# One attention and channel-mix kernel on one core: a new order of all engines, new buffer places, and casts moved to GpSimd

## The chip, the core and the metric

The kernel runs on one core of a Trainium2 chip. The core has five instruction streams that run side by side and meet through semaphores: TensorE (PE, matrix products; its weight loads are listed as PEld), VectorE (DVE), ScalarE (ACT), GpSimd (POOL) and SyncE (SP), which here issues nearly all transfers. Each stream runs its instructions in the order in which they were emitted; an instruction that waits holds up everything behind it on the same stream.

The metric is the device time of one execution in microseconds (us). The kernel before took 166.66 us, the median of three runs (166.03 to 167.26).

## The reference: what is computed

Windowed attention with a few sink keys, then an RWKV channel mix on its output, for 4 batches, 8 heads, 768 positions and heads of 64.

```python
scores = (1 / sqrt(64)) * q @ k.T
keep = (key < 4) | ((0 <= query - key) & (query - key < 128))
a = softmax(where(keep, scores, -1e9))
x = concat_heads(a @ v)                      # (4, 768, 512)
...
x_prev = x shifted by one position, 0 at the start
xk = mu_k * x + (1 - mu_k) * x_prev          # xr likewise with mu_r
k = relu(xk @ w_k)                           # 512 -> 1024
v = (k * k) @ w_v                            # 1024 -> 512
out = sigmoid(xr @ w_r) * v
```

Inputs and output are float32; the kernel computes its products in bfloat16.

## The kernel before, in words

The 4 x 768 positions are cut into 12 units of 256 positions, three to a batch (U = 12; T is the unit's place in its batch). Each unit goes through four stages.

*prepare* (lines 531 to 684). SP loads 256 positions of q, k and v in float32 (lines 307, 317 and 337, two transfers of 256 KB for each tensor). Each half is cast to bfloat16: `kb` and `qb` (op at line 547; the copies at lines 536 and 543), `vb` (op at line 648, copy at line 646). The halves of q and k are then transposed, either on PE (line 576) with a copy out of PSUM (line 589), or, for k of units 4 to 11 and q of units 8 to 11, by a DMA transpose that SP issues (line 562). For the first unit of a batch the four sink keys are gathered (`ksink`, POOL, line 670), and the sink values as well (lines 676 and 680).

*attend* (lines 687 to 828). For each pair of heads PE makes scores (line 721), ACT the exponential (line 775), DVE the product with a window mask (line 789); units 0 and 1 have the mask added on PE instead (line 728, from `bias`). PE multiplies with v (line 808, sink part at line 763), DVE takes the reciprocal of the sums (line 822) and scales (line 825) into `x`.

*mix* (lines 831 to 897). `x` is transposed on PE (line 849, copied out at line 858) or by DMA (units 9 to 11, line 869). DVE forms the difference to the position before (`td`, line 877) and from it `xk` and `xr` (line 888).

*ffn* (lines 927 to 1015). PE makes the keys (line 939), which go through a relu (ACT line 949 or DVE line 953) and a square (DVE line 963 or ACT line 967), the gate (line 979, ACT tanh at line 985) and the values (line 997); DVE joins both (line 1006) and SP stores. The last 128 positions are cut in two (lines 909 to 924). The weights are loaded once (line 354) and cast in ten pieces (lines 501, 505 and 507).

None of this is emitted as it is written. `Plan.op` only notes each of the 1052 operations with its number; `Plan.run` then emits them in the order of a written list, `ORDER`. Since each engine is in order, `ORDER` sets the order on every engine and in SP's queue. A negative entry is a filling matmul on zeros (line 1018), which does no work of the kernel and keeps PE active. `SLOTS` says, in order of the operations, which buffer of its pool each tile takes. `CHOICE` says which engine runs an operation that several engines can run (220 of the operations: casts, copies out of PSUM, relus and squares); one that is not listed stays on the engine that its `P.op` names.

```python
if i in CHOICE:
    engine = CHOICE[i]
    cost, emit, port = alts[engine]
...
for i in ORDER:
    if i < 0:
        self.fill(banks[(-1 - i) % len(banks)], 512 if -i <= len(banks) else 128)
    else:
        self.ops[i]["emit"]()
```

Numbers that the change and the prediction speak of: 0 to 3 are the loads of q and k of unit 0, 8 and 9 those of q of unit 1, 10 and 11 the loads of w_k, 82 to 89 POOL's constants (82 the identity, 87 the head mask, 88 the sink sums, 84 and 83 the biases), 92 to 101 the casts of the weights, 249 the first scores of unit 2, 212 the second transpose of x of unit 1, and 219 and 223 key products of unit 0's ffn. `TOGETHER`, `KD`, `QD`, `XD`, `BIAS` and the other settings are the same before and after.

Of the kernel before, what the change touches and what calls it, by code (L numbers as in the profile page):

```python
# [18 lines left out]
    92: "ACT", 93: "ACT", 94: "ACT", 95: "ACT", 97: "ACT", 100: "ACT", 102: "DVE", 105: "DVE",  # L19
    110: "DVE", 111: "DVE", 114: "ACT", 115: "DVE", 139: "POOL", 142: "POOL", 145: "POOL", 148:  # L20
    "DVE", 150: "DVE", 151: "ACT", 152: "ACT", 154: "DVE", 161: "DVE", 191: "DVE", 193: "DVE",
    194: "DVE", 197: "DVE", 199: "DVE", 200: "DVE", 203: "DVE", 204: "DVE", 213: "DVE", 230:
    "ACT", 234: "ACT", 273: "DVE", 276: "DVE", 279: "DVE", 282: "DVE", 285: "ACT", 286: "ACT",
    298: "DVE", 306: "DVE", 315: "ACT", 354: "DVE", 364: "ACT", 365: "DVE", 367: "DVE", 383:
    "ACT", 387: "ACT", 436: "DVE", 439: "DVE", 444: "DVE", 445: "DVE", 467: "ACT", 475: "ACT",
    514: "DVE", 516: "DVE", 521: "DVE", 524: "ACT", 525: "ACT", 546: "ACT", 550: "ACT", 554:
    "ACT", 558: "ACT", 595: "DVE", 598: "DVE", 603: "ACT", 604: "ACT", 606: "DVE", 634: "ACT",
    681: "DVE", 682: "DVE", 691: "DVE", 700: "ACT", 704: "ACT", 708: "ACT", 755: "DVE", 759:
    "DVE", 760: "ACT", 772: "DVE", 781: "ACT", 785: "ACT", 789: "ACT", 834: "DVE", 836: "DVE",
    837: "DVE", 853: "ACT", 856: "DVE", 857: "ACT", 860: "DVE", 861: "ACT", 904: "DVE", 906:  # L30
    "DVE", 910: "DVE", 912: "DVE", 913: "DVE", 929: "ACT", 933: "ACT", 940: "DVE", 941: "ACT",
    994: "DVE", 995: "ACT", 999: "ACT", 1003: "ACT", 1007: "ACT", 1022: "DVE", 1026: "DVE",
    1034: "DVE", 1035: "ACT",
# [1041 lines left out]
```

## Time and profile before

| what | value |
|---|---|
| median of three runs | 166.66 us (166.03 to 167.26) |
| span of the profiled execution, first to last instruction | 164.3 us |
| that execution's own time | not on the page; the three runs lie 1.7 to 3.0 us above the span |
| ACT casts of q, k and v | 31, of 0.62 to 0.77 us on the mean by group |
| DVE casts of q, k and v | 38, about 0.42 us each |
| POOL casts of q, k and v | 3, all between 12 and 16 us |
| filling matmuls | 30 |
| DMA, mean over the span | 211 GB/s |

A row of a group names the line, the engine, the operation, what it writes and reads, and the count; then the busy time in us and the mean of one in ns; then the engine's idle time ahead of it and what ended it. A row of the timeline begins with the start and the length in us; several instructions of the same kind in a row are merged, with their count. The chain of waits is followed back from the last instruction: each piece is what the next had to wait for. A row of stages gives, for each engine, the busy time within that stretch and the instructions in it.

### The profile page before, as it was taken

What the parts mean: (1) busy time and instruction counts of PE and PEld (TensorE: products, weight loads), DVE (VectorE), ACT (ScalarE), POOL (GpSimd) and SP (SyncE); (2) the same over time, 40 slices, a digit from 0 to 9 for tenths busy, and PEclk for the clock granted to TensorE, in tenths of its full rate; (3) what the DMA queues carried; (4) which work ended last, traced back from release to release, by engine and by line L of the source; (5) the groups of instructions that cost most, each with busy time, mean ns of one, the idle gap of its engine ahead of it and who ended that gap; (6) DMA issues with size and microseconds to landing.
All of it is one profiled execution on the core that took longest, in us unless ns stands there. A gap on an engine that the chain in (4) does not pass through costs nothing.

```text
span 164.3 us, 4195 instructions
## 1 busy us (share of the span) xinstructions
PE 158.4 (96%) x1603; PEld 102.6 (62%) x1603; DVE 145.4 (89%) x381; ACT 131.2 (80%) x218; POOL 13.5 (8%) x38
## 2 busy tenths in 40 slices
PE   6999889999999999999999999999999999999992
PEld 2455568866467587577566775856575765664851
DVE  5259999999999999989999999999999999789752
ACT  3277999999999999999999999997668759163240
POOL 6409300010000000060000000000000000000000
PEclk9999999999999999999999999999999999999999
DMA  4999999999969896999999887986996955077743
GB/s 120 247 305 311 348 335 355 301 354 210 228 154 270 135 240 148 234 198 167 224 216 157 188 156 163 235 146 150 199 123 136 362 149 200 0 90 297 262 185 128
DMA packets 79042, 34.60 MB, mean 211 GB/s; under 512 B 67112, under 2 KB 73520, under 8 KB 79024
## 3 DMA queue, kind: packets, MB, share of 16 engines
q1 hardware_dynamic: 79008, 34.35, 86.3%
q8 instruction: 12, 0.20, 0.6%
q14 instruction: 6, 0.05, 0.1%
q10 hardware_dynamic: 16, 0.00, 0.0%
HBM read 24.12 MB, written 6.29 MB: 185 GB/s over the span
## 4 chain that ended last, share of the span: by engine, by line
PE 79%; ACT 8%; SPq 4%; DMA 3%; issue 2%; DVE 1%; POOL 1%; DVEq 0%; ACTq 0%; POOLq 0%
PE bank L997 23%; PE bank L939 23%; PE bank L979 12%; PE bank L808 6%; PE sc L721 6%; SPq L337 3%; DMA qs<-in_q_dram 3%; PE bank L576 2%; ACT e L775 2%; PE bank L849 2%; ACT rl L949 1%; PE bank L763 1%; ACT qt L589 1%; PE bank L909 1%; PE bank L1018 1%
## 5 line engine op out<-in xcount | busy, mean ns | idle before, releaser
L775 ACT ACTIVATE e<-sc 128x1024 bf16<-128x1024 f32 (+1 forms) x48 | 46.1, 994 | 1.8 <-PE sc L721 1.7
L939 PE MATMUL bank<-xk,wk_sb 128*128 128x256 bf16 x384 | 47.1, 273 | 0.0
L997 PE MATMUL bank<-wv_h,kk 128*128 128x512 bf16 x184 | 43.1, 379 | 0.1
L939 PEld LDWEIGHTS <-wk_sb 128*128 128x128 bf16 x384 | 36.4, 98 | 7.4 <-issue 0.4
L949 ACT ACTIVATE rl<-bank 128x512 bf16<-128x512 f32 x40 | 24.2, 625 | 8.6 <-PE bank L939 7.1
L997 PEld LDWEIGHTS <-kk 128*128 128x128 bf16 x184 | 17.1, 98 | 17.8 <-issue 0.4
L789 DVE TENSOR_TENSOR e<-e,mask 128x1024 bf16<-128x1024 bf16 (+1 forms) x40 | 25.4, 642 | 0.7 <-ACT e L775 0.5
L979 PE MATMUL bank<-wr_sb,xr 128*128 128x512 bf16 x96 | 23.7, 379 | 0.0
L888 DVE SCALAR_TENSOR_TENSOR xk<-td,mu_all,xt 128x256 bf16<-128x256 bf16 x48 | 22.4, 483 | 0.3
L888 DVE SCALAR_TENSOR_TENSOR xr<-td,mu_all,xt 128x256 bf16<-128x256 bf16 x48 | 22.1, 475 | 0.2
L967 ACT ACTIVATE kk<-rl 128x512 bf16<-128x512 bf16 x29 | 18.3, 664 | 4.2 <-DVE rl L953 4.0
L985 ACT ACTIVATE th<-bank 128x512 f32<-128x512 f32 x24 | 15.1, 646 | 5.7 <-PE bank L979 5.7
L825 DVE TENSOR_TENSOR x<-bank,rec 128x256 bf16<-128x256 f32 x48 | 19.2, 416 | 0.4
L808 PE MATMUL bank<-vb,e 128*128 128x65 bf16 x352 | 16.6, 194 | 0.0
L1006 DVE SCALAR_TENSOR_TENSOR w<-th,bank 128x512 f32<-128x512 f32 x19 | 13.0, 682 | 3.6 <-issue 1.8
L808 PEld LDWEIGHTS <-e 128*128 128x128 bf16 x352 | 13.6, 97 | 3.5
L979 PEld LDWEIGHTS <-xr 128*128 128x128 bf16 x96 | 8.8, 98 | 8.6 <-issue 0.2
L721 PE MATMUL sc<-qt,kt 64*128 64x128 bf16 (+1 forms) x256 | 13.9, 238 | 0.0
L721 PEld LDWEIGHTS <-kt 64*128 64x128 bf16 x256 | 8.9, 94 | 5.7 <-issue 3.1
L1018 PE MATMUL bank<-warm 128*128 128x512 bf16 x30 | 10.6, 484 | 1.1 <-DVE warm L1038 1.1
L877 DVE TENSOR_TENSOR td<-xt 128x512 bf16<-128x512 bf16 x24 | 10.3, 428 | 0.7 <-ACT xt L858 0.5
L589 ACT COPY qt<-bank 128x512 bf16<-128x512 bf16 x15 | 9.4, 643 | 1.0 <-PE bank L576 1.0
(74 smaller groups left out, 161.7 us busy)
## 6 DMA issues: line engine op xcount, KB each, us to landing
ks<-in_k_dram SPq DMA_DIRECT2D x24, 256.0 KB, 4.7
qs<-in_q_dram SPq DMA_DIRECT2D x24, 256.0 KB, 4.4
vs<-in_v_dram SPq DMA_DIRECT2D x24, 256.0 KB, 4.4
out_dram<-w SPq DMA_DIRECT2D x19, 256.0 KB, 2.7
w<-in_moe_w_k_dram SPq DMA_DIRECT2D x2, 1024.0 KB, 10.4
w<-in_moe_w_v_dram SPq DMA_DIRECT2D x2, 1024.0 KB, 9.3
w<-in_moe_w_r_dram SPq DMA_DIRECT2D x1, 1024.0 KB, 9.7
out_dram<-ob SPq DMA_DIRECT2D x4, 256.0 KB, 2.6
```

What stands on the lines that cost most here:

```text
L721: nc.tensor.matmul(out=sc[:, a, o0:o1], lhsT=lhs[rows], rhs=rhs[rows], start=u not in BIAS, stop=True, skip_group_check=u in BIAS)
L775: nc.scalar.activation(out=buf[ek][:, :, lo:], in_=buf[sck][:, :, lo:], func=AF.Exp, scale=scale)
L789: nc.vector.tensor_tensor(out=at, in0=at, in1=m, op=ALU.mult)
L808: nc.tensor.matmul(out=o[:, g, a, :], lhsT=e[:, a, e0:e0 + 128], rhs=rhs, start=(T == 0 and i == 0), stop=(i == len(blocks) - 1), skip_gro ...
L825: P.op("DVE", dve(256), lambda ok=ok, rk=rk, c=c: nc.vector.tensor_tensor(out=buf["x", u][:, :, 128 * c:128 * c + 128].rearrange("p g (a d ...
L888: nc.vector.scalar_tensor_tensor(out=buf[key][:, c, :], in0=buf[tk][:, i, :], scalar=mu[w][:, c:c + 1], in1=xt[:, c, t0 - 1:t0 + 255], op0 ...
L939: nc.tensor.matmul(out=ps[:, i, :], lhsT=wk_sb[:, c, 128 * f:128 * f + 128], rhs=xk[:, c, :], start=(c == 0), stop=(c == NC - 1), skip_gro ...
L949: nc.scalar.activation(out=buf[rk], in_=buf[psk].rearrange("p (i t) -> p i t", i=2), func=AF.Relu)
L967: nc.scalar.activation(out=buf["kk", u][:, 2 * f2:2 * f2 + 2, :], in_=buf[rk], func=AF.Square)
L979: nc.tensor.matmul(out=buf[psk], lhsT=buf["xr", u][:, c, 128 * g:128 * g + 128], rhs=wr_sb[:, c, :], start=(c == 0), stop=(c == NC - 1))
L985: P.op("ACT", act(512), lambda psk=psk, tk=tk: nc.scalar.activation(out=buf[tk], in_=buf[psk], func=AF.Tanh, scale=0.5), rank + 4 + g, tak ...
L997: nc.tensor.matmul(out=buf[psk], rhs=wv_h[:, f, :], lhsT=buf["kk", u][:, f, 128 * g:128 * g + 128], start=(f == 0), stop=(f == NF - 1))
```

## The change

Only the three lists are replaced. No operation is added or removed, apart from filling matmuls, of which there are 21 instead of 30.

- `CHOICE` now names all 220 operations. Those on POOL go from 3 to 55: 52 casts of q, k and v (3 before) and 3 casts of weights (none before). ACT goes from 31 to 8 casts of q, k and v, and from 6 to 3 of weights; DVE from 38 to 12 casts of q, k and v. Relus on ACT go from 40 to 42, squares on ACT from 29 to 31, copies of x on ACT from 10 to 8, copies of q and k out of PSUM on ACT from 20 to 19; DVE has the rest of each.
- `ORDER` is new throughout. SP's loads begin with q of unit 0, then its k, then half of q of unit 1; the w_k loads stay 17th and 18th. POOL begins with the head mask and ends its first five jobs with the identity. Operations 249 and 212 now stand ahead of the first key product.
- `SLOTS` is new, to fit the order.

```diff
 CHOICE = {
-    92: "ACT", 93: "ACT", 94: "ACT", 95: "ACT", 97: "ACT", 100: "ACT", 102: "DVE", 105: "DVE",
-    110: "DVE", 111: "DVE", 114: "ACT", 115: "DVE", 139: "POOL", 142: "POOL", 145: "POOL", 148:
...
+    92: "ACT", 93: "POOL", 94: "ACT", 95: "POOL", 96: "DVE", 97: "POOL", 98: "DVE", 99: "DVE",
+    100: "ACT", 101: "DVE", 102: "DVE", 104: "ACT", 105: "POOL", 107: "DVE", 108: "DVE", 110:
+    "ACT", 111: "DVE", 113: "DVE", 114: "POOL", 115: "DVE", 139: "POOL", 141: "ACT", 142: "ACT",
...
 ORDER = (
-    80, 81, 78, 82, 87, 83, 84, 77, -1, -2, -3, -4, -1, -2, 90, 0, 1, 79, 102, 108, -2, -3, -4,
-    -2, -3, -4, -2, 103, 104, 2, 3, 119, 105, -3, -4, 106, 107, 109, 110, 4, 5, 114, -2, -2, -2,
...
+    80, 87, 81, 88, 84, 83, 82, 77, 2, 3, 0, 1, 8, 4, 79, 78, -1, -2, -3, -4, -1, -2, -3, -4, -1,
+    -2, -3, -4, 119, 5, 105, 111, 106, 102, 108, 103, 112, 104, 107, 113, -4, 120, 121, 85, 114,
...
 SLOTS = (
-    0, 0, 0, 1, 1, 0, 1, 1, 2, 0, 1, 2, 2, 2, 0, 0, 0, 1, 1, 1, 2, 2, 0, 0, 0, 2, 1, 1, 1, 2, 2,
...
+    0, 0, 0, 1, 1, 0, 1, 1, 2, 0, 1, 2, 2, 2, 0, 0, 0, 1, 1, 1, 2, 2, 0, 0, 0, 2, 1, 1, 1, 2, 0,
...
 )
```

More of the change, by code (lines that the diff above doesn't have):

```diff
@@ L18 @@
 CHOICE = {
-    92: "ACT", 93: "ACT", 94: "ACT", 95: "ACT", 97: "ACT", 100: "ACT", 102: "DVE", 105: "DVE",
-    110: "DVE", 111: "DVE", 114: "ACT", 115: "DVE", 139: "POOL", 142: "POOL", 145: "POOL", 148:
[L21 to L30, printed above, removed]
@@ new lines @@
+    144: "DVE", 145: "POOL", 147: "ACT", 148: "DVE", 150: "ACT", 151: "POOL", 152: "POOL", 154:
+    "DVE", 161: "DVE", 191: "POOL", 193: "ACT", 194: "POOL", 196: "ACT", 197: "POOL", 199: "ACT",
+    200: "POOL", 202: "ACT", 203: "POOL", 204: "POOL", 206: "DVE", 213: "ACT", 221: "ACT", 222:
+    "DVE", 225: "ACT", 226: "ACT", 229: "DVE", 230: "DVE", 233: "DVE", 234: "ACT", 273: "POOL",
+    275: "DVE", 276: "POOL", 278: "ACT", 279: "POOL", 281: "ACT", 282: "POOL", 284: "ACT", 285:
+    "ACT", 286: "POOL", 291: "DVE", 298: "ACT", 306: "DVE", 307: "ACT", 310: "ACT", 311: "ACT",
@@ new lines @@
+    314: "ACT", 315: "ACT", 318: "ACT", 319: "DVE", 354: "ACT", 356: "POOL", 358: "ACT", 359:
+    "POOL", 361: "ACT", 363: "ACT", 364: "POOL", 365: "POOL", 367: "DVE", 374: "ACT", 382: "ACT",
+    383: "DVE", 386: "ACT", 387: "ACT", 390: "ACT", 391: "ACT", 394: "ACT", 395: "DVE", 434:
+    "POOL", 436: "DVE", 438: "ACT", 439: "POOL", 441: "DVE", 443: "DVE", 444: "ACT", 445: "POOL",
+    447: "DVE", 454: "ACT", 462: "ACT", 463: "ACT", 466: "ACT", 467: "ACT", 470: "ACT", 471:
+    "DVE", 474: "ACT", 475: "ACT", 514: "POOL", 516: "POOL", 518: "ACT", 519: "POOL", 521: "POOL",
@@ new lines @@
+    523: "ACT", 524: "POOL", 525: "POOL", 530: "DVE", 537: "DVE", 545: "ACT", 546: "ACT", 549:
+    "ACT", 550: "ACT", 553: "ACT", 554: "ACT", 557: "DVE", 558: "ACT", 593: "POOL", 595: "POOL",
+    597: "ACT", 598: "POOL", 600: "POOL", 602: "ACT", 603: "POOL", 604: "POOL", 606: "ACT", 613:
+    "ACT", 621: "ACT", 622: "DVE", 625: "ACT", 626: "DVE", 629: "ACT", 630: "DVE", 633: "ACT",
+    634: "ACT", 673: "ACT", 675: "DVE", 677: "POOL", 679: "POOL", 681: "POOL", 682: "POOL", 684:
+    "ACT", 691: "ACT", 699: "ACT", 700: "DVE", 703: "ACT", 704: "ACT", 707: "ACT", 708: "ACT",
@@ new lines @@
+    711: "ACT", 712: "ACT", 751: "POOL", 753: "POOL", 755: "POOL", 757: "DVE", 759: "POOL", 760:
+    "POOL", 765: "DVE", 772: "DVE", 780: "ACT", 781: "ACT", 784: "ACT", 785: "ACT", 788: "ACT",
+    789: "DVE", 792: "ACT", 793: "DVE", 828: "POOL", 830: "POOL", 832: "DVE", 834: "POOL", 836:
+    "POOL", 837: "ACT", 852: "ACT", 853: "ACT", 856: "ACT", 857: "ACT", 860: "ACT", 861: "DVE",
+    864: "ACT", 865: "ACT", 904: "POOL", 906: "DVE", 908: "POOL", 910: "POOL", 912: "ACT", 913:
+    "DVE", 928: "ACT", 929: "DVE", 932: "ACT", 933: "ACT", 936: "ACT", 937: "ACT", 940: "ACT",
@@ L34 @@
+    941: "ACT", 994: "ACT", 995: "DVE", 998: "ACT", 999: "DVE", 1002: "ACT", 1003: "ACT", 1006:
+    "ACT", 1007: "DVE", 1022: "ACT", 1023: "ACT", 1026: "ACT", 1027: "ACT", 1030: "DVE", 1031:
+    "ACT", 1034: "DVE", 1035: "ACT",
 }
```

3 lines of the change are left out of this document (removed), and 152 rows, old and new, of tables (ORDER, SLOTS).

## The prediction

> **What bounds the kernel now.** I read the page's first part, then busy time by stage, then the chain of waits, then the groups of TensorE (PE) work, and last the places where GpSimd (POOL) and VectorE (DVE) meet.
>
> ```profile
> span 164.3 us, 4195 instructions
> PE 158.4 (96%) x1603; PEld 102.6 (62%) x1603; DVE 145.4 (89%) x381; ACT 131.2 (80%) x218; POOL 13.5 (8%) x38
> ```
>
> ```profile
> core 0: us, PE busy (x) PEld busy (x) DVE busy (x) ACT busy (x) POOL busy (x), PEclk, DMA share, GB/s
> 0.00:24.00 24.00, 21.48 (x217) 11.69 (x218) 16.75 (x54) 16.31 (x26) 9.86 (x32) 1.00 0.94 277
> 24.00:60.00 36.00, 35.96 (x384) 24.66 (x385) 35.40 (x93) 35.70 (x59) 0.74 (x2) 1.00 0.98 253
> 60.00:110.00 50.00, 49.89 (x562) 34.03 (x559) 47.82 (x128) 49.57 (x88) 2.89 (x4) 1.00 0.97 187
> 110.00:161.00 51.00, 51.00 (x445) 32.24 (x443) 45.00 (x109) 29.61 (x49) 0.00 (x0) 1.00 0.69 176
> ```
>
> Two stages: a start of 24 us, in which nothing but attention of the first units runs, and from 24 to 161 us a stretch in which PE is never idle (35.96 of 36, 49.89 of 50, 51.00 of 51). ACT is as full up to 110 us, DVE nearly. A busy PE need not be PE at its peak, since matmuls overlap, so I check with the chain, which shows what runs back to back, and with the counts in that stretch.
>
> ```profile
> 27.01 2.73 PE bank L939 x24
> 29.74 0.22 PE bank L576 x4
> ...
> 32.81 0.55 PE sc L721 x12
> ...
> 33.47 0.59 PE bank L808 x16
> ...
> 36.09 1.73 PE bank L979 x8
> ```
>
> ```profile
> L939 PE MATMUL bank<-xk,wk_sb 128*128 128x256 bf16 x384 | 47.1, 273 | 0.0
> L997 PE MATMUL bank<-wv_h,kk 128*128 128x512 bf16 x184 | 43.1, 379 | 0.1
> L979 PE MATMUL bank<-wr_sb,xr 128*128 128x512 bf16 x96 | 23.7, 379 | 0.0
> L808 PE MATMUL bank<-vb,e 128*128 128x65 bf16 x296 | 13.6, 194 | 0.0
> L721 PE MATMUL sc<-qt,kt 64*128 64x128 bf16 (+1 forms) x216 | 11.6, 237 | 0.0
> ```
>
> Back to back a 256-column matmul takes 2.73/24 = 0.114 us, a 512-column one 1.73/8 = 0.216, a value matmul 0.59/16 = 0.037, a score matmul 0.55/12 = 0.046. Times the counts: 384 x 0.114 + (184 + 96) x 0.216 + 296 x 0.037 + 216 x 0.046 = 43.8 + 60.5 + 11.0 + 9.9 = 125 us, and the small transposes (0.22 for four) and sink products fill the other 12. So these 137 us hold 137 us of PE work at full rate. The change keeps every matmul, so it can shorten this stretch by next to nothing. It can gain only in the first 24 us, and it can lose anywhere.
>
> **The change part by part: the casts.** Counted in the two lists, POOL runs 3 of the selectable operations before and 55 after: 49 more casts of q, k or v and 3 of weights, 52 in all (the title's 27 is not what the lists hold). Of the 49, ACT loses 23 and DVE 26. Besides, ACT takes 2 relus and 2 squares from DVE, and DVE a net 2 copies of x and 1 of q or k from ACT.
>
> ```profile
> L536 ACT CAST kb<-ks 128x512 bf16<-128x512 f32 x10 | 6.6, 655 | 0.0
> L646 DVE CAST vb<-vs 128x512 bf16<-128x512 f32 x13 | 5.4, 420 | 0.1
> L543 DVE CAST qb<-qs 128x512 bf16<-128x512 f32 x11 | 4.6, 416 | 2.3 <-DMA qs<-in_q_dram 2.3
> L501 ACT ACTIVATE wk_sb<-w 128x1024 bf16<-128x1024 f32 x4 | 4.2, 1092 | 0.0
> ```
>
> ACT is freed of 23 x 0.66 + 3 x 1.09 = 18.5 us, DVE of 26 x 0.42 = 10.9; the small exchanges, under 3 us either way, move within the room so made. Between 60 and 73 us the chain runs over ACT, yet PE works 49.89 of 50 us there: a freer ACT shortens nothing that PE does not set. Both gains count as 0 and are cover.
>
> What the casts cost on POOL is seen where before has them beside DVE work.
>
> ```profile
> 12.64 0.86 POOL L543 CAST qb<-qs 128x512 bf16<-128x512 f32 x1 [6.67 <-DMA qs<-in_q_dram]
> 13.48 0.62 POOL L543 CAST kb<-ks 128x512 bf16<-128x512 f32 x1
> ...
> 15.01 0.79 POOL L543 CAST kb<-ks 128x512 bf16<-128x512 f32 x1
> 15.74 0.55 POOL L470 COPY vsink<-hmask 128x8 bf16<-128x8 bf16 x2
> 16.20 0.44 POOL L670 COPY ksink<-kt 64x16 bf16<-64x16 bf16 x2
> ```
>
> ```profile
> 13.75 0.62 DVE L877 TENSOR_TENSOR td<-xt 128x512 bf16<-128x512 bf16 x1
> ...
> 15.34 0.73 DVE L888 SCALAR_TENSOR_TENSOR xk<-td,mu_all,xt 128x256 bf16<-128x256 bf16 x1
> ```
>
> ```profile
> L888 DVE SCALAR_TENSOR_TENSOR xk<-td,mu_all,xt 128x256 bf16<-128x256 bf16 x48 | 22.4, 483 | 0.3
> ...
> L877 DVE TENSOR_TENSOR td<-xt 128x512 bf16<-128x512 bf16 x24 | 10.3, 428 | 0.7 <-ACT xt L858 0.5
> ```
>
> The cast takes 0.62 us in the best of the three cases, 0.79 and 0.86 in the others, so it comes on the mean 0.14 late ((0 + 0.17 + 0.24)/3). The two DVE instructions that met one took 0.19 and 0.25 us longer than their groups' means (0.62 for 0.43, 0.73 for 0.48): they end 0.27 us after the cast does. POOL and DVE hold each other up. Over 52 casts, DVE then pays about 52 x 0.22 = 11.4 us, which eats the 10.9 it was freed of; its idle time of 36 - 35.40 + 50 - 47.82 = 2.8 us between 24 and 110 us stays as it is. Ends of this price: 0, and a whole cast each, 52 x 0.62 = 32 us, which the 11 freed and 2.8 idle would not cover. I take 0.22, the value of the two rows of the very pair of operations, so DVE costs nothing net, with no cover left.
>
> PE is in order, so a late cast costs time where its transpose or value product stands close behind it. I walked both lists and added up the PE work, by the prices above, that is issued between a POOL cast and PE's first use of it. After the start there are 12 casts with under 1 us of it (kb or qb of units 3, 4 and 7, vb of units 3, 4, 6, 8 and 9, and three weight casts). On ACT or DVE such a cast took its known time; on POOL it is 0.14 us late by the three casts: 12 x 0.14 = **1.7 us**. The other end is the one POOL operation of before that met a run of DVE work.
>
> ```profile
> 70.30 2.54 POOL L670 COPY ksink<-kt 64x16 bf16<-64x16 bf16 x2 [36.96 <-DMA kt<-kb]
> ```
>
> ```profile
> 70.25 0.42 DVE L646 CAST vb<-vs 128x512 bf16<-128x512 f32 x1
> 70.59 0.42 DVE L543 CAST qb<-qs 128x512 bf16<-128x512 f32 x1
> 70.93 0.41 DVE L963 TENSOR_TENSOR kk<-rl 128x512 bf16<-128x512 bf16 x1
> 71.26 1.28 DVE L789 TENSOR_TENSOR e<-e,mask 128x1024 bf16<-128x1024 bf16 x2
> ```
>
> Two tiny copies, 0.44 us elsewhere, took 2.54, and end when the fifth DVE instruction in a row does (72.54): 2.1 us late. Mean over this and the three casts: (0 + 0.17 + 0.24 + 2.1)/4 = 0.63, so 12 x 0.63 = 7.6 us at the upper end; at the lower end 0, if the room on ACT lets all other work run ahead. I take the rows of the same instruction, the casts.
>
> The Trainium skill, "SBUF — State Buffer", section Who interferes with whom, says that the port pair shared by GpSimd and VectorE is an exclusive lock, held for a whole instruction, against VectorE instructions in a two-port mode or with two SBUF inputs. The rows at 13.75 and 15.34 agree. By that rule no cast waits for more than the one DVE instruction in front of it; the row at 70.30 waited for five, so the measurement speaks for worse than the rule. With half a mask product (0.32 us) for each of the 12 the sum would be 3.8 instead of 1.7 us.
>
> **The start.** Unit 0's q goes to places 1 and 2 of SP's loads, its k to 3 and 4; unit 1's q moves from places 8 and 9 to 5 and 8, its first half ahead of unit 0's v and both ahead of its own k. The weights stay at 17 and 18, behind the same 16 loads.
>
> ```profile
> 7.61 0.43 DVE L543 CAST qb<-qs 128x512 bf16<-128x512 f32 x1 [2.31 <-DMA qs<-in_q_dram]
> ```
>
> ```profile
> 7.31 1.28 SPq L337 DMA_DIRECT2D qs<-in_q_dram  x2
> ```
>
> ```profile
> 7.97 4.54 DMA qs<-in_q_dram
> ```
>
> Scores need both, and whichever is fourth lands at 7.6 us: q ahead of k is worth 0 by itself. Worth something is unit 1's q: the chain waits for it from 7.97 to 12.51 us, and it now stands one place earlier, 1.28/2 = 0.64 us by the issue times. Against it, the identity, which every transpose reads, is now the last of POOL's first five jobs, not the first.
>
> ```profile
> 5.65 0.32 POOL L451 COPY spread<-ident 4x16 bf16<-4x16 bf16 x2
> ```
>
> ```profile
> 7.04 0.39 PE L576 MATMUL bank<-ident,kb 128*128 128x128 bf16 x4
> ```
>
> Four of these jobs are over at 5.65 us now; the fifth, the two copies at 15.74, adds 0.55, so the identity is there by 6.2 us or little later, and the first transposes stood at 7.04 anyway: 0. First-unit masks and casts queue on POOL, where a cast of unit 1's k stands behind one of v. Nine of 30 filling matmuls go; they were issued where PE had nothing else. Two more attention steps stand ahead of the first L939 matmul, 0.55 + 0.22 = 0.8 us of work that the stretch of 137 us no longer holds. Ends: 0 (POOL's queue eats it), and 2.1, the 1.3 us to the landing of an earlier place plus that 0.8. I take **0.7 us**, the one place.
>
> SP's order changes in 24 transposing DMAs too, most of whose casts are now POOL's; loads behind them wait as they do now, several units ahead, so I cost this at 0; without that lead a late cast would add its 0.14 us to a load. Buffer places change with the order and are costed with it. The end is the same four products and two stores: 0.
>
> **Sum.** Against the profiled execution: 164.3 - 0.7 + 1.7 = 165.3 us of span. The runs shown lie 1.7 to 3.0 us above that span, their median 2.4 (166.66 - 164.3): 165.3 + 2.4 = **167.7 us**.
>
> **Rivals.** *Slower.* POOL casts wait through runs of DVE work, as at 70.30. At half of the upper end, 3.8 us, the time is 166.66 - 0.7 + 3.8 = 169.8; at the full end 173.6. It decides when a tight cast comes over 0.2 us late (1.7 + 0.7 = 2.4 us over 12), close to the 0.14 that I take. For it: DVE is 96 to 98% busy up to 110 us. Against it: DVE has copies from PSUM and reciprocals among its work, and the cast at 13.48 slipped in beside one. *Faster.* The start gives all of 2.1 us and no cast is late: 164.6. For it: ACT gains 18.5 us of room, and the first weights no longer have to be cast by ACT alone. Against it: weights land no earlier. *No effect of the load order*, 166.66 + 1.7 = 168.4, lies beside the forecast and counts half to each side of it.
>
> **How the numbers follow.** About 1% (1.7 us) is what a measurement of this kernel can tell from no change: 165.0 to 168.3. Forecast with its neighbours 0.46, slower 0.41, faster 0.13. These are also the chances of within 1%, slower and faster. The range runs from 164.8, near the best start, to 172, between the half and the full end of the late casts, leaving out about 0.07 below and 0.12 above; the likeliest case alone would be 165.0 to 168.3.
>
> **What would show it.** Right: PE still full from its first L939 matmul to the end; POOL casts of 0.6 to 0.9 us; xk, xr and td rows on the mean longer by about 0.1 us; ACT with ten or more idle us before 110. The start is right if the first L939 matmul comes at 23 to 24 us with unit 2's first scores ahead of it. Wrong: PE idle or its weight loads waiting for POOL kb, qb or vb by more than 2 us in total, POOL casts of over 1 us (slower), or the first L939 matmul before 22.7 us (faster). A lower PEclk after the start would show that the missing fill counts after all.

## The result, and the profile after

The changed kernel takes 172.43 us (median of four runs, 171.16 to 174.5), the kernel before 166.51 on the same chip (median of four as well): 1.034 times as long, with a 95% interval of 1.028 to 1.039. The ratio leaves out the run at 174.5 us, which was a slow one. The 5.9 us are a clear loss. The forecast was 167.7 us, and its range ended at 172.0. The profiled executions have spans of 170.7 and 164.3 us; TensorE's last product ends at 167.5 us, 6.4 later than before.

The head of the page and the start of its chain, after:

```profile
span 170.7 us, 4204 instructions
...
PE 159.2 (93%) x1594; PEld 102.1 (60%) x1594; DVE 146.5 (86%) x354; ACT 119.5 (70%) x193; POOL 49.0 (29%) x90
...
PE 41%; DVE 17%; DMA 15%; SPq 9%; ACT 8%; POOL 5%; issue 3%; POOLq 0%; DVEq 0%; ACTq 0%
```

ACT is freed of 11.7 us (131.2 to 119.5), less than the 18.5 counted: in the kernel before a cast on ACT follows the last at about 0.53 us where its row says 0.66, since rows of one engine overlap. DVE's busy time moves by only 1.1 us (145.4 to 146.5). Yet the chain, on PE for 79% of its length before, is on PE for 41% now; DVE, loads and SP's queue hold the rest. The stages, with the columns of before:

```profile
24.00:60.00 36.00, 34.08 (x350) 22.56 (x348) 35.39 (x77) 29.76 (x50) 12.34 (x18) 1.00 0.97 246
60.00:110.00 50.00, 48.16 (x524) 32.53 (x523) 48.57 (x117) 39.75 (x65) 18.88 (x28) 1.00 1.05 199
110.00:130.00 20.00, 18.36 (x198) 11.69 (x197) 16.72 (x42) 12.80 (x22) 3.29 (x5) 1.00 0.87 193
130.00:161.00 31.00, 31.00 (x273) 20.03 (x270) 24.73 (x64) 20.47 (x35) 0.00 (x0) 1.00 0.41 132
```

PE is idle 1.9 us in the first of these, 1.8 in the second, 1.6 in the third: 5.4 us where the kernel before had 0.15. After 130 us, when the last cast is done, it is full again. Counted from the matmul records (a hole is what lies between the starts of two matmuls beyond the back-to-back time of the first), before has one hole of over 0.25 us after 24 us (0.28 us), after has twelve, 7.2 us together: 2.7 us up to 50 us, 2.7 from there to 108, and 1.8 at 115. Less the 0.8 us of work that the start takes over, that is the 6.4 us at the end. Seven of the holes end with a DVE instruction whose last wait was for no load (3.0 us together), one with DVE behind a load (1.8), one with a POOL cast of v behind a load (0.6), three with ACT (1.8). The loss is in these holes, and what the experiments have to say is who makes them.

The start came as forecast, as a time. The first key product of the ffn begins at 23.89 us (23.98 before), and now unit 2's first scores and one more transpose of x, 0.8 us of work, lie ahead of it:

```profile
23.65 0.40 PE L862 MATMUL bank<-ident,x 128*128 128x128 bf16 x4
23.89 0.60 PE L952 MATMUL bank<-xk,wk_sb 128*128 128x256 bf16 x4
```

Right behind it PE has two holes, 0.7 us at 26 before a cast of w_k and 0.3 at 28 before an xk, which pay the gain back.

DVE's groups, by form (the lines are 13 further down than before):

```profile
L901 DVE SCALAR_TENSOR_TENSOR xk<-td,mu_all,xt 128x256 bf16<-128x256 bf16 x48 | 27.2, 587 | 0.2
L901 DVE SCALAR_TENSOR_TENSOR xr<-td,mu_all,xt 128x256 bf16<-128x256 bf16 x48 | 24.2, 520 | 0.1
...
L802 DVE TENSOR_TENSOR e<-e,mask 128x1024 bf16<-128x1024 bf16 x28 | 19.8, 717 | 0.1
```

These were 483, 475 and 681 ns. With td (428 to 454), the narrow mask products (550 to 584) and one weight cast (1.10 us), the lengthening comes to 9.6 us, 0.19 for each POOL cast: close to the 0.22 of the forecast. How it reaches PE is seen at the hole at 107 us (0.5 us). A row gives start, length and, in brackets, what the engine waited for:

```profile
105.73 0.68 DVE L1019 SCALAR_TENSOR_TENSOR w<-th,bank 128x512 f32<-128x512 f32 x1
106.33 0.74 DVE L901 SCALAR_TENSOR_TENSOR xk<-td,mu_all,xt 128x256 bf16<-128x256 bf16 x1
107.00 0.24 DVE L835 RECIPROCAL rec<-bank 128x4 f32<-128x4 f32 x2
107.27 0.76 DVE L838 TENSOR_TENSOR x<-bank,rec 128x256 bf16<-128x256 f32 x2
107.75 1.02 PE L992 MATMUL bank<-wr_sb,xr 128*128 128x512 bf16 x4 [0.35 <-DVE x L838]
```

DVE is busy 8.63 of the 8.70 us up to 107.3, and the xk at 106.33 took 0.74 us beside a POOL cast (106.18 to 106.79). No load stands in this chain. The hole of 1.8 us at 115 us, the largest, is of the other kind:

```profile
115.86 0.43 DVE L549 CAST kb<-ks 128x512 bf16<-128x512 f32 x1 [2.01 <-DMA ks<-in_k_dram]
116.20 0.48 DVE L901 SCALAR_TENSOR_TENSOR xr<-td,mu_all,xt 128x256 bf16<-128x256 bf16 x1
116.60 0.55 DVE L802 TENSOR_TENSOR e<-e,mask 128x768 bf16<-128x768 bf16 x1
...
117.21 0.36 PE L821 MATMUL bank<-vb,e 128*128 128x65 bf16 x6 [1.64 <-DVE e L802]
```

DVE stands 2.01 us before a cast whose load has not landed; the mask that PE needs is third in that queue. PE's wait is written down to DVE, but what DVE waited for is a load.

Matching the loads of both kernels by their place in SP's queue shows which moved. Start of the issue, us:

| load | before | after |
|---|---|---|
| second half of k, units 8, 9, 10 | 71.1, 83.2, 101.1 | 80.6, 92.1, 110.4 |
| second half of v, units 5 and 9 | 60.0, 101.7 | 70.7, 110.0 |
| first half of q, units 9 and 11 | 82.6, 112.5 | 72.0, 100.1 |
| first half of k, unit 11; of v, unit 10 | 102.6, 109.9 | 92.7, 99.4 |

**Theory A, the port**: POOL's casts and DVE's instructions hold each other up, and DVE's delay reaches PE. **Theory B, the loads**: in the new order some loads come later, and engines stand in line before them. Out of the runs came **theory C**: both, by turns, so that relief from one is eaten by the other.

### The profile page after: what moved, and what is told of

Its sections match the earlier page's. It is cut to its first block, busy times and chain, and to the rows that moved or that the text cites. A ratio compares the mean times of both kernels' runs of the same rounds, so it can differ in the third digit from the quotient of the medians.

```text
span 170.7 us, 4204 instructions
## 1 busy us (share of the span) xinstructions
PE 159.2 (93%) x1594; PEld 102.1 (60%) x1594; DVE 146.5 (86%) x354; ACT 119.5 (70%) x193; POOL 49.0 (29%) x90
## 4 chain that ended last, share of the span: by engine, by line
PE 41%; DVE 17%; DMA 15%; SPq 9%; ACT 8%; POOL 5%; issue 3%; POOLq 0%; DVEq 0%; ACTq 0%
PE bank L952 14%; PE bank L1010 11%; DMA ks<-in_k_dram 10%; PE bank L992 7%; ACT e L788 5%; DVE xk L901 5%; SPq L350 4%; DMA qs<-in_q_dram 3%; PE bank L821 3%; DVE e L802 3%; SPq L320 2%; DMA vs<-in_v_dram 2%; PE sc L734 2%; DVE xr L901 2%; DVE x L838 2%
## 5 line engine op out<-in xcount | busy, mean ns | idle before, releaser
L952 PE MATMUL bank<-xk,wk_sb 128*128 128x256 bf16 x384 | 49.3, 272 | 1.1 <-ACT wk_sb L514 0.5
L788 ACT ACTIVATE e<-sc 128x1024 bf16<-128x1024 f32 (+1 forms) x48 | 44.1, 955 | 3.5 <-PE sc L734 3.4
L1010 PE MATMUL bank<-wv_h,kk 128*128 128x512 bf16 x184 | 44.4, 379 | 0.0
L962 ACT ACTIVATE rl<-bank 128x512 bf16<-128x512 f32 x42 | 24.9, 598 | 16.8 <-PE bank L952 10.4
L901 DVE SCALAR_TENSOR_TENSOR xk<-td,mu_all,xt 128x256 bf16<-128x256 bf16 x48 | 27.2, 587 | 0.2
L802 DVE TENSOR_TENSOR e<-e,mask 128x1024 bf16<-128x1024 bf16 (+1 forms) x40 | 26.9, 677 | 0.3 <-ACT e L788 0.2
L901 DVE SCALAR_TENSOR_TENSOR xr<-td,mu_all,xt 128x256 bf16<-128x256 bf16 x48 | 24.2, 520 | 0.1
L998 ACT ACTIVATE th<-bank 128x512 f32<-128x512 f32 x24 | 14.2, 600 | 12.0 <-PE bank L992 12.0
L659 POOL CAST vb<-vs 128x512 bf16<-128x512 f32 x18 | 12.5, 695 | 22.1 <-DMA vs<-in_v_dram 18.1
L549 POOL CAST kb<-ks 128x512 bf16<-128x512 f32 x13 | 10.2, 788 | 25.5 <-DMA ks<-in_k_dram 19.3
L992 PEld LDWEIGHTS <-xr 128*128 128x128 bf16 x96 | 8.8, 98 | 10.5 <-issue 1.0
L1019 DVE SCALAR_TENSOR_TENSOR w<-th,bank 128x512 f32<-128x512 f32 x17 | 11.4, 678 | 1.6 <-PE bank L1010 1.5
```

The source lines that it names most:

```text
L788: nc.scalar.activation(out=buf[ek][:, :, lo:], in_=buf[sck][:, :, lo:], func=AF.Exp, scale=scale)
L802: nc.vector.tensor_tensor(out=at, in0=at, in1=m, op=ALU.mult)
L901: nc.vector.scalar_tensor_tensor(out=buf[key][:, c, :], in0=buf[tk][:, i, :], scalar=mu[w][:, c:c + 1], in1=xt[:, c, t0 - 1:t0 + 255], op0 ...
L952: nc.tensor.matmul(out=ps[:, i, :], lhsT=wk_sb[:, c, 128 * f:128 * f + 128], rhs=xk[:, c, :], start=(c == 0), stop=(c == NC - 1), skip_gro ...
L962: nc.scalar.activation(out=buf[rk], in_=buf[psk].rearrange("p (i t) -> p i t", i=2), func=AF.Relu)
L992: nc.tensor.matmul(out=buf[psk], lhsT=buf["xr", u][:, c, 128 * g:128 * g + 128], rhs=wr_sb[:, c, :], start=(c == 0), stop=(c == NC - 1))
```

## The experiments

**Old tables and new ones mixed.** The first two runs took one table from each kernel.

```diff
-CHOICE = {...}                 # the change's
+CHOICE = {...}                 # that of before; ORDER and SLOTS as in the change
```

> Order and buffer places of the changed kernel, engines as before (3 casts on GpSimd). Theory A (the GpSimd casts and VectorE hold each other up at a shared port, and VectorE's delay reaches TensorE): xk, xr and mask rows fall back to about 0.48, 0.48 and 0.68 us, and the time to 165 to 167.5 us. Theory B (the new order brings loads late, and engines wait for them in order, whichever engine casts): the waits for loads stay, and so does the time, 170 to 174 us.

```diff
-ORDER = (...); SLOTS = (...)   # the change's
+ORDER = (...); SLOTS = (...)   # those of before; CHOICE as in the change
```

> Order and buffer places of before, engines of the change (55 operations on GpSimd). Theory A: xk rows of 0.55 to 0.6 us and 170 to 175 us, since the port costs the same in any order. Theory B: no load comes later than before, so 166 to 168 us.

Measured: 198.52 us (1.191, 1.186 to 1.196) and 190.34 us (1.144, 1.139 to 1.149). Both theories missed both, by 15 us and more. An order is written for a choice of engines: with the new engines in the old order, POOL stands before a load for up to 10.5 us (5.5 in the changed kernel), and PE has eighteen holes, 18.8 us together, that end with ACT or DVE. That the one makes the other is likely but was not followed. These two runs cannot share out the loss.

**The new start alone**: the change's order and engines up to its first key product, before's from there on.

```diff
-ORDER = (...)                  # the change's
+ORDER = (80, 87, 81, ..., up to the first ffn operation, then the rest in before's order)
...                             # CHOICE likewise; SLOTS new, to fit
```

> The changed kernel's order and engines up to the first key product of the ffn, the order and engines of before after it. Both theories: only the start differs from before, so the time is that of before less what the start gains, 0.9 us by the two traces (first key product at 23.9 instead of 24.0 us with 0.8 us of attention more ahead of it): 165.6 us. If the start's gain is only work put off (casts and mixing of unit 1 that the rest still has to do), 166.5 or above.

Measured: 167.19 us (1.005, 1.003 to 1.008), by the second forecast. The start is worth nothing. In the joined order more attention stands ahead of the first key product, which comes at 25.05 us, and around it PE waits for DVE's x and for the cast weights (engine, line and what it waited for: us in total, times, longest):

```profile
PE bank L591 <- DVE x L840: 0.7, 2, 0.5
PE bank L954 <- ACT wk_sb L516: 0.5, 1, 0.5
```

What PE does earlier, it pays back by waiting for the same weights and the same DVE. The loss of 5.9 us is not made in the start.

**The port, measured on the kernel before**: 48 casts whose result nobody reads, two behind each tanh, and then fills in their place.

```diff
+    P.extra = lambda th: nc.gpsimd.tensor_copy(out=extra16, in_=th)
...
                 self.ops[i]["emit"]()
+                if key and key[0] == "th":
+                    self.extra(self.buf[key])
+                    self.extra(self.buf[key])
```

> The kernel of before with 48 extra GpSimd casts (128x512, float32 to bfloat16) of which nobody uses the result, two behind each tanh of the gate. No order, load or cast of the kernel changes. Theory A: VectorE pays about 0.2 us for each, 9.6 us in all, xk and xr rows rise by 0.05 us or more on the mean, and the time by 3 to 8 us, 170 to 174 us. Theory B: 166.5 to 167 us.

```diff
-    P.extra = lambda th: nc.gpsimd.tensor_copy(out=extra16, in_=th)
+    def extra(th):
+        nc.gpsimd.tensor_copy(out=extra16[0:1, 0:1], in_=th[0:1, 0:1])
+        nc.gpsimd.memset(extra16, 0.0)
```

> The kernel before with 48 unused pairs on GpSimd, at the places of the 48 unused casts: a copy of one element of the tanh tile, then a fill of 128x512 bf16. They wait for the same tanh, and the sink copies queue behind them just the same, so the some 4 us that the casts cost by that stay. Port theory: VectorE's rows keep their 0.483, 0.475 and 0.681 us, busy time stays near 145.4 us, and the time is 169.5 to 172 us, 6 to 8 under that with the casts (177.95). Rival (what costs is the place on GpSimd's queue and not the port): 176 to 178 us.

Measured: 177.95 us with casts (1.069, 1.065 to 1.073), 175.69 with fills (1.058, 1.055 to 1.061). DVE's groups by form, with casts:

```profile
L892 DVE SCALAR_TENSOR_TENSOR xk<-td,mu_all,xt 128x256 bf16<-128x256 bf16 x48 | 24.7, 532 | 0.3
L892 DVE SCALAR_TENSOR_TENSOR xr<-td,mu_all,xt 128x256 bf16<-128x256 bf16 x48 | 24.0, 514 | 0.2
L793 DVE TENSOR_TENSOR e<-e,mask 128x1024 bf16<-128x1024 bf16 x28 | 20.0, 723 | 0.1
```

and with fills:

```profile
L892 DVE SCALAR_TENSOR_TENSOR xk<-td,mu_all,xt 128x256 bf16<-128x256 bf16 x48 | 22.4, 484 | 0.3
L892 DVE SCALAR_TENSOR_TENSOR xr<-td,mu_all,xt 128x256 bf16<-128x256 bf16 x48 | 22.2, 476 | 0.2
...
L793 DVE TENSOR_TENSOR e<-e,mask 128x1024 bf16<-128x1024 bf16 x28 | 18.9, 682 | 0.3 <-ACT e L779 0.2
```

With fills the rows are those of before; with casts DVE is busy 155.2 instead of 145.7 us, 0.20 us a cast. So it is the casts that lengthen DVE's instructions, and not a busy POOL. The Trainium skill, "SBUF — State Buffer", section Who interferes with whom, says that a VectorE instruction with two SBUF inputs contends with a GpSimd instruction that reads SBUF, and not with one that only writes it; the 532 against 484 ns agree.

The casts cost more than either theory had, and the fills lie over the port theory's 172 and just under the rival's 176. In the time the two runs differ by only 2 us (11.6 and 9.6 us over before on each run's own chip), but that is not the port's price. PE's waits, with casts:

```profile
PE bank L700 <- POOL ksink L674: 2.9, 1, 2.9
PE bank L1001 <- DVE wv_h L509: 1.6, 1, 1.6
...
PE bank L943 <- DVE x L829: 1.0, 1, 1.0
```

and with fills, PE's and the DVE wait behind its second:

```profile
PE bank L700 <- POOL ksink L674: 3.2, 1, 3.2
PE bank L580 <- DVE ob L1010: 3.1, 1, 3.1
DVE e L793 <- POOL mask L438: 3.8, 1, 3.8
```

With casts PE has holes of 10.4 us: 3.0 behind sink copies that stand in POOL's line after the free casts, and 6.8 that end with DVE. With fills it has 7.4: 3.4 behind the sink copies, 3.8 behind a mask that POOL makes after the first free pairs, and none else that ends with DVE. The pairs hold POOL for longer than the casts (0.93 against 0.81 us; the first eight 9.9 against 6.9 us in all), so the mask comes 2.4 us later. The fills took away the 6.8 us of DVE and brought in the 3.8. Both things cost here: the port, and a place in an engine's line.

**Fills in the changed kernel.**

```diff
+    def pool_fill(out, in_):
+        at = (slice(0, 1),) * len(out.shape)
+        nc.gpsimd.tensor_copy(out=out[at], in_=in_[at])
+        nc.gpsimd.memset(out, 0.0)
...
-                       "POOL": (600.0, cast(nc.gpsimd.tensor_copy), True)},
+                       "POOL": (600.0, cast(pool_fill), True)},
```

> The changed kernel with each of GpSimd's casts of q, k and v replaced by a copy of one element (which keeps the wait for the load) and a fill of the whole bf16 tile with zeros; so q, k and v are not really cast there, and the two fills of 0.3 us for 256 columns in the trace of before say that a fill of 512 takes some 0.6 us, about as long as the cast. A fill reads nothing from SBUF. Port theory (a cast on GpSimd and VectorE's instructions hold each other up, and VectorE's delay reaches TensorE): VectorE's rows go back towards 0.483 us (xk), 0.475 (xr) and 0.681 (the mask), and the time falls by most of the 5.9 us, to 166 to 168 us. Load theory (the new order makes loads late, and POOL, VectorE and the SP queue wait for them one behind the other): waits for loads stay, and the time stays at 171 to 173 us.

```diff
-        nc.gpsimd.memset(out, 0.0)
+        nc.gpsimd.memset(out[:, 0:out.shape[1] // 2], 0.0)
...
-                       "POOL": (600.0, cast(pool_fill), True)},
+                       "POOL": (600.0, cast(pool_fill if u > 2 else nc.gpsimd.tensor_copy), True)},
```

> The changed kernel with GpSimd's casts of q and k from unit 3 on, and of v from unit 4 on, replaced by a copy of one element (which keeps the wait for the load) and a fill of half the tile: those q, k and v are not cast. The copy took 0.34 us and the fill of 512 columns 0.53 with the whole fills, so the pair takes about 0.61 us, no longer than the 0.65 to 0.79 us of a cast, and the start is left as it is (the whole fills made it 1.4 us later). Port theory: 24 to 60 us loses 1.7 us of TensorE's gaps as with the whole fills, the later stretches 1.8, and nothing is given back at the start: 168 to 169.5 us. Load theory: the waits for loads close behind the faster VectorE, 171 to 172.5 us.

Measured: 172.19 us (1.036, 1.033 to 1.039) and 172.23 us (1.035, 1.031 to 1.039): no gain, as the load theory had it. And yet DVE was relieved (busy 139.9 instead of 146.5 us). With fills throughout, by form:

```profile
L908 DVE SCALAR_TENSOR_TENSOR xk<-td,mu_all,xt 128x256 bf16<-128x256 bf16 x48 | 22.2, 484 | 0.2
...
L809 DVE TENSOR_TENSOR e<-e,mask 128x1024 bf16<-128x1024 bf16 x28 | 18.9, 682 | 0.1
```

Runs with the same order on PE and ACT can be laid side by side: the n-th of ACT's 114 large activations (exponentials, relus, tanhs) does the same work in each. Start against that of the changed kernel, us (minus is earlier; the runs of the last four columns are told further down, "refitted" is the second attempt at SP's order):

| after's time | short fills | SP in order of need + short fills | SP refitted + short fills | SP refitted | 4 loads earlier |
|---|---|---|---|---|---|
| 46.1 | -0.4 | -0.6 | -0.7 | +0.7 | +0.9 |
| 86.3 | -1.6 | -2.2 | -2.2 | +0.4 | +1.1 |
| 108.8 | -3.3 | -3.9 | -3.9 | +0.3 | +1.3 |
| 117.4 | +1.0 | +4.5 | -3.7 | +0.9 | +1.4 |
| 131.1 | -0.8 | +2.6 | -4.4 | -1.0 | +0.5 |
| 158.5 | -0.8 | +2.6 | -2.9 | -1.0 | +0.5 |

Each column is a single execution. The two runs without fills have the changed kernel's orders up to 60 us and still lie 0.7 and 0.9 us behind at 46, so less than about 1 us says nothing. Between 117 and 131 us each column moves in its favour by what it has not of the changed kernel's own hole at 115.

The short fills run ahead steadily, 3.3 us by 108 us, and lose 4.3 between 109 and 117. SP's line in that stretch, short fills:

```profile
100.35 2.52 SPq L337 DMA_DIRECT2D qs<-in_q_dram  x3
102.91 1.01 SPq L1033 DMA_DIRECT2D out_dram<-ob  x1
104.03 1.24 SPq L582 DMA_TRANSPOSE kt<-kb  x1
105.31 0.58 SPq L337 DMA_DIRECT2D qs<-in_q_dram  x1
105.99 1.21 SPq L582 DMA_TRANSPOSE kt<-kb  x1
```

The scores wait for the transposed second half of unit 9's k. The fill that stands for its cast is done at 95.93 us, but its transposing DMA, the last row, stands in SP's line behind loads and a store, and lands at 109.61. The hole is 2.6 us, and it costs 1.7 more: stages with the whole fills, which have the same hole (the granted clock is the third number from the end; its shortfall in the last three rows, 0.31, 0.50 and 0.04 of 2 us each, is 1.7 us):

```profile
107.40:110.00 2.60, 0.28 (x4) 0.09 (x2) 1.08 (x3) 0.14 (x1) 0.83 (x3) 1.00 1.15 208
110.00:112.00 2.00, 1.99 (x31) 1.61 (x32) 0.59 (x3) 1.55 (x3) 0.00 (x0) 0.69 0.95 229
112.00:114.00 2.00, 2.00 (x8) 0.98 (x7) 1.68 (x5) 1.97 (x4) 0.77 (x3) 0.50 1.22 253
114.00:116.00 2.00, 2.00 (x13) 1.05 (x12) 0.74 (x3) 0.00 (x0) 1.24 (x4) 0.96 0.90 193
```

**Loads moved, in the changed kernel.** First the second halves of twelve loads right behind their first, alone and with the whole fills; then four loads; then the whole old sequence of loads.

```diff
 SP:  load k 8 first half
+     load k 8 second half
...
-     load k 8 second half        # likewise for k of units 6, 9 to 11, q of 8, 9 and 11, v of 5, 9 to 11
```

> The changed kernel with the second half of twelve loads of q, k and v (units 5, 6 and 8 to 11) issued right behind its first half on SP, and nothing else moved. Load theory: the wait of VectorE for the second half of unit 10's k (2.01 us, with a hole of 1.8 us in TensorE at 115) goes, GpSimd's waits for k fall well under 19 us, and the time falls by 2 us or more, to 168 to 170 us. Port theory: only the hole at 115 goes, the other loads are not what TensorE waits for; 170.5 to 172.5 us, VectorE's rows unchanged at 0.587, 0.520 and 0.677.

> Both edits at once on the changed kernel: fills for GpSimd's casts of q, k and v (which are then not cast), and the second halves of twelve loads issued at once. Port theory: about the time of the fills alone, 165.5 to 167.5 us. Load theory: about the time of the second halves alone, 168 to 170 us. If both count, the two gains add.

Measured: 174.41 us (1.050, 1.046 to 1.054) and 175.13 us (1.055, 1.051 to 1.059), both outside all that was expected: slower than the change. The chain up to the largest hole of the first (1.9 us at 82.5):

```profile
76.28 1.11 SPq L332
...
79.69 1.16 SPq L322
...
80.97 1.42 SPq L577
...
82.50 2.44 DMA kt<-kb
```

SP issues without a pause there; what is put ahead pushes transposes back.

```diff
 SP:  load v 5 first half
+     load v 5 second half
...
      transpose q 9 second half
+     load q 10 first half, q 10 second half, k 10 second half
      load v 10 first half, q 11 first half
-     load q 10 first half, q 10 second half
...                                # v 5 and k 10 second half go from their old places
```

> The changed kernel with four loads issued earlier on SP, and nothing else: the second half of unit 5's v right behind its first half, both halves of unit 10's q ahead of the loads of unit 10's v and unit 11's q, and the second half of unit 10's k right behind them. These are the loads at the head of the chains that end in TensorE's holes at 75, 107 and 115 us (loads of 3.66, 5.45 and 5.31 us in them). Load theory, in the form that a few late loads do it: those three holes (0.6, 0.5 and 1.8 us, with smaller ones about them some 4 us) go, and the time falls to 168.5 to 170.5 us. Port theory, in the form that VectorE is the bound in 24 to 110 and a hole that goes opens again behind VectorE: 171 to 173 us.

Measured: 172.24 us (1.035, 1.031 to 1.040). The port theory's second form, as far as the time goes: the hole at 115 shrinks to 0.9 us, others come with DVE as their end. (The hole at 107 us that the expectation puts down to a load of 5.45 us ends a chain over DVE alone, as shown above; that load leads to the hole at 115.)

> The changed kernel with the loads on SP in the sequence of before (the places in the queue that hold a load stay, and which load stands in each is that of before); transposes, stores, all other engines and the choice of engines are those of the change. The slots of the buffers are given out anew where that order needs it. Load theory: the sequence of loads is what costs, so 167 to 170 us. Port theory: 171 to 173 us. A third way, after the kernels of before's and after's tables mixed whole (190 and 198 us): the casts stand in the order of the new loads, so that a sequence that doesn't fit them makes GpSimd and VectorE wait at the head of their queues, over 175 us.

(ORDER alone is edited: the loads in before's sequence. The buffer places stay those of the change, so waits for buffers may be part of it.) Measured: 179.84 us (1.081, 1.079 to 1.083), the third way. DVE waits 6.5 us before one cast of q, and PE has a hole of 5.5 us.

**Two bounds at once.** SP's line in the order of need (with unit 5's v as in the run of four loads), with short fills and without.

```diff
 SP:  transpose q 9 second half
+     load q 10 first half, q 10 second half, k 10 second half
+     transpose k 9 second half, k 10 first half
+     load v 9 second half
      load v 10 first half, q 11 first half
-     load q 10 first half, q 10 second half
      store
-     transpose k 10 first half
      load q 11 second half
-     transpose k 9 second half
...
-     load v 9 second half, k 10 second half
```

> The changed kernel with short fills in place of GpSimd's casts of q and k from unit 3 and of v from unit 4 on (which are then not cast), and with SP's queue put in the order of need at 97 to 117 us: both halves of unit 10's q and the second half of its k, then the transposes of unit 9's k (second half) and unit 10's k, then the second half of unit 9's v, and only then the loads of unit 10's v and unit 11's q and the store that stood among them; the second half of unit 5's v goes right behind its first. With the short fills alone the work was 3.3 us ahead of the changed kernel at 108 us and 1.0 behind it at 117, after a hole of 2.6 us in which the key products waited for unit 9's k. Theory C (two bounds that take turns: VectorE slowed by the port up to 108 us, then SP's queue at 107 to 117; either alone hides the relief of the other): the 3.3 us stay to the end, 168.3 to 170 us. Port theory alone: as the short fills alone, 171.5 to 172.5. Load theory alone: as the queue order alone.

> The changed kernel with that same order of SP's queue, and all casts as in the change. Theory C: VectorE still holds the work back up to 108 us, and SP's queue no longer does behind it; of the some 2.5 us of holes at 107 to 117 one or two come back: 170 to 172 us. Load theory alone: 168 to 170 us. Port theory alone: 171.5 to 173 us.

Measured: 175.56 us (1.057, 1.053 to 1.061), slower than all that was expected, and 172.74 us (1.038, 1.035 to 1.041), where the port theory alone had it and not theory C. With short fills the lead is 3.9 us at 109 us, and then 8.4 are lost. DVE's rows, with short fills:

```profile
104.33 0.68 DVE L809 TENSOR_TENSOR e<-e,mask 128x1024 bf16<-128x1024 bf16 x1
111.75 0.43 DVE L556 CAST qb<-qs 128x512 bf16<-128x512 f32 x1 [6.73 <-issue]
112.09 0.68 DVE L809 TENSOR_TENSOR e<-e,mask 128x1024 bf16<-128x1024 bf16 x1
```

The row names no releaser, but the cast of unit 11's q starts 0.08 us after that load lands (111.67): moving this load back was the error, and the mask of unit 9 stood behind its cast. So this load goes ahead again:

```diff
 SP:  transpose q 9 second half
+     load q 11 first half
      load q 10 first half, q 10 second half, k 10 second half
      transpose k 9 second half, k 10 first half
      load v 9 second half
-     load v 10 first half, q 11 first half
+     load v 10 first half
```

> As the run with SP's queue in the order of need and short fills (175.56 us), but the first load of unit 11's q stays ahead of the loads moved, since VectorE's cast of it stands in its queue ahead of the masks of unit 9: in that run the load landed at 111.7 us, VectorE stood before the cast, and TensorE had a hole of 5.7 us behind a lead of 3.9 us. Theory C (two bounds that hide each other: VectorE slowed by the port, and casts at the head of VectorE's and GpSimd's queues that wait for their loads): the lead of 3 to 4 us at 108 us is kept, 168 to 170 us. Rival (any order of the loads makes another cast wait, the loads cannot be brought in by then at all): a new hole of over 2 us at 105 to 118, 171 us or more.

> The changed kernel with that order of SP's queue and all casts as in the change. Theory C: the work is not early at 108 us, so that only the holes behind late loads (1.8 us at 115 and part of those at 107) come back: 170 to 172 us. Rival (loads alone): 168 to 170.

Measured: 170.07 us (1.023, 1.021 to 1.026) and 171.38 us (1.030, 1.028 to 1.033), on one chip. Theory C's forecasts, the first 0.1 us over its upper end. Fills are worth 1.3 us here, and the intervals do not touch; with the loads unfitted they were worth nothing that shows. Against the run beside it the lead is 4.2 us at 109, 3.4 at 131 and 1.9 at the end; 1.5 us of it go between 131 and 137. The chain ahead of that, in the run with fills:

```profile
124.32 1.14 SPq L889
125.51 2.66 DMA xt<-x
...
128.26 0.78 DVE td L897 x2
```

A DMA transpose of x on SP's line is next: it is issued at 124.14 us, only 1.0 us earlier than in the run beside it, where the work is 3.4 us earlier or more, and DVE waits 1.8 us for it. For SP's fit alone (171.38 against 172.43) the intervals overlap (1.028 to 1.033 and 1.028 to 1.039), though the hole at 115 us is gone.

**Two casts taken from DVE**, no load moved:

```diff
-    832: "DVE",
+    832: "POOL",
...
-    906: "DVE",
+    906: "POOL",
```

> The changed kernel with two casts given from VectorE to GpSimd, at the same places of the order: unit 10's k, second half, for which VectorE waits 2.01 us ahead of a mask, and unit 11's q, first half. No load is moved. If the hole of 1.8 us at 115 us is VectorE standing at the head of its queue before a load: that hole goes, 170 to 171.5 us. If VectorE's work is what bounds and the wait only fills its slack: 172 to 173 us.

> The same two casts given to GpSimd, with the short fills (so that GpSimd's q and k from unit 3 and v from unit 4 on are not cast). With the short fills alone a hole of 2.6 us at 107 (key products behind the transposes of unit 9's k) and one of 1.7 at 115 (VectorE before unit 10's k) ate a lead of 3.3 us. Theory C: the second of them goes, the first stays; 170 to 171 us. Rival (loads alone bound, port without effect): as the same two casts with real casts.

Measured: 173.4 us (1.043, 1.040 to 1.046) and 172.38 us (1.038, 1.034 to 1.042). No gain, both outside what was expected of theory C, and the first 0.4 us over what was expected of its rival too. With real casts one wait takes the place of DVE's:

```profile
PE bank L823 <- POOL vb L661: 2.8, 1, 2.8
```

The cast that waits for unit 10's k now stands in POOL's line ahead of the cast of v that PE needs. The wait moved from one queue to another. With fills the hole of unit 9's k stays as expected (2.7 us), and PE waits 1.0 us for that v.

## Why the prediction was wrong

- **The step that failed: DVE "costs nothing net, with no cover left".** The sum came near: 0.19 against 0.22 us a cast, busy time up by 1.1 us. There was luck in it, as both its sides were too large: back to back, DVE's casts follow each other at 0.34 us (70.25, 70.59, 70.93 in the prediction's rows), so 26 of them free 8.8 us and not 10.9. But it is a sum of busy time, and PE waits for single tiles. PE had next to no wait in this stretch before (0.15 us of idle time), so taking casts off DVE gained nothing; the xk, xr and mask rows grew longer, and what DVE makes reaches PE late: seven holes, 3.0 us. Relieving DVE brought the work 3.3 to 3.9 us ahead by 109 us, of the 5.4 us of holes up to there. At the end of the kernel the runs show 1.3 us of it at most, since the next bound follows closely. In the old order 48 casts made 6.8 us of holes behind DVE.
- **The step beside it: SP's order "costed at 0", the loads "several units ahead".** They were not. Five second halves of k and v came 8 to 11 us later, and the holes at 75 and 115 us (2.4 us together) end chains that run over a load (3.7 and 5.3 us of it). The rule that a late cast's delay adds to a load does show once: ahead of the hole at 75 us a POOL cast of k of 1.98 us holds up SP's transposing DMA and the load of v behind it. For the hole at 115 it asked the wrong question: not how late a load is, but which cast stands first in line before it, and what stands behind that cast.
- **Late casts, 1.7 us**: PE's own waits for POOL's casts are two of 0.5 us, 1.0 in all, under the mark of 2 us. A size near the right one by another path: most of POOL's cost reaches PE through DVE.
- **The slower rival** holds the measured time between its 169.8 and 173.6 us, but mostly by luck. Its mark was a cast over 0.2 us late; the 52 casts took 0.73 us on the mean, 0.11 over the 0.62 of the best row: 45 took 0.60 to 0.81, six 0.90 to 1.08, one 1.98. That one, at 67.45 us, did wait through a run of DVE work, two masks and a td. What POOL waited for was otherwise loads: 19.3 us for k and 18.1 for v.
- **The start, 0.7 us**: right as a time at 24 us, and worth nothing by itself (167.19 us).
- **"PE still full to the end"** failed at once: 5.4 us idle in 24 to 130 us. The working that PE works 137 of 137 us showed that nothing could be gained there. I read it as a floor and not as a warning that each wait of any other engine would show in full. The clock had no part in the loss: 1.00 in every stage of the changed kernel from 24 us on.

What stays open: after both reliefs 3.9 of the 5.9 us remain (170.07). They lie in ten holes of 0.28 to 0.96 us, 4.8 us together, behind a weight cast, DVE, transposing DMAs of k and of x. None was taken away by itself; nor were the three weight casts on POOL or the new buffer places tried alone. How the loss is shared between port and loads has no single answer either, as each hides part of the other; shown in the time are 1.3 us for the port with the loads fitted, none that shows without, and about 1 us, not told from 0, for the fitted loads alone.

## What to carry to other kernels

In a kernel whose engines all run in a written order, a cast's price is not only its duration: ask what it lengthens on other engines, which load it waits for, and what stands behind it in its line. When two engines are near full, relief of one shows up at a milestone in the middle and not in the time; lay runs side by side by the same operation to see where a lead is made and where it is lost. Tables of order and of engines are one thing: taken apart they cost 24 and 32 us over the kernel before.

## What the runs showed of the hardware

TensorE's clock. After holes of 2.5, 2.6, 3.0 and 5.7 us the granted clock went to 0.50 for three to five us, which after the 2.6 us came to 1.7 us more (4.3 lost in all). After holes of 1.8 and 1.9 us (changed kernel, and second halves at once) it stayed at 1.00, and once also after 3.0 us (two casts taken from DVE):

```profile
115.00:118.40 3.40, 0.61 (x15) 0.35 (x12) 1.66 (x3) 2.92 (x5) 2.51 (x6) 1.00 0.60 122
118.40:120.00 1.60, 1.60 (x12) 0.76 (x10) 1.33 (x4) 0.00 (x0) 1.60 (x3) 1.00 0.41 82
```

The Trainium skill, "TensorE: Matmul & The Clock Gate", Part 1: The HAM clock gate (the "warmup" mystery), gives an idle window of about 3.4 us before the clock is halved. Half speed agrees with the rows. The length does not: here a hole of 2.5 us was enough, and one of 3.0 once was not.

A small POOL operation beside a busy DVE. With whole fills a copy of a single element on POOL took 0.18 us at best and 0.34 on the mean, a fill of 128x512 0.53, the whole cast in the changed kernel 0.60 at best and 0.73 on the mean. In the kernel before with 48 fills one such copy took 2.56 us, from 36.94 to 39.50, while DVE ran a cast, a mask, two weight casts and a square in a row: as in the prediction's row at 70.30, a POOL operation can wait through several DVE instructions, and not only through the one in front of it.
